# Packed attention with a SoLU MLP: the output stores move from the queue of SyncE to the queue of ScalarE

## The chip, the cores and the metric

The kernel runs on one core of a Trainium2 chip. The metric is the device time of one execution in microseconds; the three runs of the kernel before gave 470.54, 470.95 and 472.06, a median of 470.95. The profile was taken from one further execution of 470.67 us.

## The reference

What must be computed, cut to its core:

```python
def sm_attn(q, k, v):            # per batch and head, scale = 1/8
    s = scale * q @ k.T
    a = exp(s - max(s)); a = a / (sum(a) + 1e-9)
    return a @ v
packed = sm_attn(p, k, v)        # 32 packed rows for each of 8 batches and 8 heads
x = sm_attn(q, packed, packed)   # 576 rows for each batch, heads side by side: (4608, 512)
h = x @ w_in                     # (4608, 1024)
solu = h * softmax(h)
ln = (solu - mean(solu)) / sqrt(var(solu) + 1e-6) * g_ln
out = ln @ w_out                 # (4608, 512), float32
```

## The kernel before

The 4608 rows of the output are made in 36 tiles of 128 rows. There are 8 batches; four or five tiles belong to each, and a tile that straddles two batches takes its rows from both. In the text the tiles and their stores are counted from 0 to 35.

For each batch two generators spread attention work between the tiles of the MLP. `pack` (from L342) makes the 32 packed rows of a head: scores (L368), softmax (L373, L381), transposes of the exponentials on TensorE (L397) that ScalarE copies out of PSUM as `e1T` (L398), and the product with `v` (L407). `unpack` (from L419) makes the second attention with the input weights folded in: scores (L467), softmax (L443 to L451), the product of packed rows and `w_in` (L483), copied by ScalarE as `zh` (L485) with its rest `zl` (L500), and the transposed probabilities `a2h` and `a2l` (L505 to L508).

The MLP of a tile has three stages, each of a different step. `mlp_in` multiplies (L521), takes the row maximum on VectorE (L523), the exponential on ScalarE (L531) and `u` on VectorE (L534). `mlp_norm` subtracts the mean: `negmu` on GpSimd (L542), the upper half of `yhl` on ScalarE (L544), the lower half on VectorE (L545), a transposing DMA of `yhl` into `yT` that SyncE's queue issues (L547), and the sum of squares on ScalarE (L549), from which GpSimd makes `c_row` (L551 to L555). `mlp_out` multiplies `yT` with the halves of `w_out` (24 matmuls, L564), VectorE scales the result into `o_sb` (L566), and a pair of output rows and `o_sb` is put on the list `stores`.

`step` (L608) puts these together: `mlp_in` of a tile, `mlp_norm` of the tile before, then `store()`, which issues a DMA for what is on the list (the tile whose `mlp_out` came in the step before), then `mlp_out` of an earlier tile. Two more calls follow at the end.

All DMAs of the kernel are issued by SyncE's queue: the loads of `q` (L85, 16 of 72 KB for each of six batches), `k` (L96, four of 288 KB) and `v` (L107 and L134, two of 512 KB and one of 128 KB), the 36 transposes and the 36 stores of 256 KB. `raw` has three buffers, `v_sb` one, and `yhl`, `yT` and `o_sb` have two each.

The order of instructions on TensorE from the second batch on is that of the program. On the other engines and on SyncE's queue a planner orders them while it plays the program through in modelled time: by priorities (the offsets of `high_priority`) among what is ready. An engine then works through its list in order, and so an instruction that waits for a semaphore holds up what is behind it in that engine's list.

Of the kernel before, what the change touches and what calls it, by code (L numbers as in the profile page):

```python
# [38 lines left out]
def packed_attention_solu_kernel(ctx: ExitStack, tc: tile.TileContext, q: bass.AP, k: bass.AP, v: bass.AP, p: bass.AP, w_in: bass.AP, w_out: bass.AP, g_ln: bass.AP, out: bass.AP):  # L39
# [13 lines left out]
    nc = tc.nc  # L53
# [514 lines left out]

    def store():
        while stores:  # L570
            nc.sync.dma_start(*stores.pop(0))

    def run(work, n=None, offset=0):
        with tc.high_priority(offset=offset):
# [31 lines left out]
    normed, summed, stores = ([], [], [])  # L606

    def step(row, parts, knobs, work):  # L608
        lag, pout, pnorm = knobs
        before, after, mid = work  # L610
        before()
        nxt = mlp_in(row, parts)
        after()
        ready = normed.pop(0) if len(normed) > lag else None
        if summed:
            with tc.high_priority(offset=pnorm):
                normed.append(mlp_norm(*summed.pop()))
        store()
        if ready:
            with tc.high_priority(offset=pout):  # L620
                mlp_out(*ready, mid)
        else:
            mid()
        summed.append(nxt)
# [37 lines left out]
    for tile_ in normed:  # L662
        mlp_out(*tile_)
    store()
_INS = ['q', 'k', 'v', 'p', 'moe_w_in', 'moe_w_out', 'moe_g_ln']
_OUTS = [((4608, 512), 'float32')]
# [23 lines left out]
```

## Time and profile before

| what | value |
|---|---|
| median of 3 runs | 470.95 us (470.54 to 472.06) |
| the profiled execution | 470.67 us, of which the span is 468.9 us |
| TensorE busy (matmul) | 430.2 us, 92% |
| VectorE busy | 354.2 us, 76% |
| ScalarE busy | 232.4 us, 50% |
| GpSimd busy | 148.0 us, 32% |
| data DMAs, share of the 16 DMA engines | 74.3% |
| chain that ended last | TensorE 58%, VectorE 18%, DMA 10%, GpSimd 5% |

The span runs from the first to the last instruction; 1.8 us of the execution's time lie outside it. Engines are shortened as PE (TensorE's matmuls), PEld (its weight loads), DVE (VectorE), ACT (ScalarE), POOL (GpSimd) and SP (SyncE); a q behind a name, as in SPq, means the queue that issues DMAs. L571 is line 571 of the kernel. "out<-in" names the tiles that an instruction writes and reads. A figure in brackets at the end of a row is the idle time of the engine ahead of the instruction, with what ended it.

### The profile page before, as it was taken

Reading aid. Unit: us, or ns where it says so; the run is one execution under the profiler, and the core shown is the slowest. Engines: PE = TensorE matmul, PEld = TensorE weight load, DVE = VectorE, ACT = ScalarE, POOL = GpSimd, SP = SyncE. Lnnn points to the kernel's source line nnn. Section 1 sums busy time; section 2 is a strip of 40 time slices with the busy share of each in tenths; the row PEclk is TensorE's granted clock in tenths of the full one; section 3 lists DMA queues with packets and bytes.
Section 4 is the critical chain, followed back from the end, with each engine's and each line's share of the span. In section 5 each row is a group of like instructions: output and inputs, shape, how many; then the busy total and the mean of one; then the engine's idle time right before and its main releaser. Section 6 shows DMA issues by size and latency. Waiting matters only on the chain.

```text
span 468.9 us, 8271 instructions
## 1 busy us (share of the span) xinstructions
PE 430.2 (92%) x3116; PEld 234.7 (50%) x3116; DVE 354.2 (76%) x648; ACT 232.4 (50%) x404; POOL 148.0 (32%) x244
## 2 busy tenths in 40 slices
PE   9697795859979999999899998999999999999995
PEld 7472244633434555446544554566445555575552
DVE  3568989778768887988489979975898688655551
ACT  3577848654343653565244562653356536433430
POOL 3424556935103211421044123311342142111220
PEclk9979759988998999999999999999999999999999
DMA  9999999999569969965989588339035333526342
GB/s 265 336 268 286 152 207 124 135 193 155 110 138 185 169 127 181 191 142 95 204 111 135 109 177 154 89 69 214 23 68 113 69 69 83 119 67 134 70 101 78
DMA packets 237880, 67.00 MB, mean 143 GB/s; under 512 B 208912, under 2 KB 231440, under 8 KB 237328
## 3 DMA queue, kind: packets, MB, share of 16 engines
q1 hardware_dynamic: 237840, 66.48, 74.3%
q8 instruction: 24, 0.39, 0.4%
q14 instruction: 16, 0.13, 0.1%
HBM read 37.23 MB, written 9.44 MB: 100 GB/s over the span
## 4 chain that ended last, share of the span: by engine, by line
PE 58%; DVE 18%; DMA 10%; POOL 5%; issue 4%; SPq 2%; ACT 2%; DVEq 0%; ACTq 0%; POOLq 0%
PE po L564 30%; PE h L521 17%; DMA yT<-yhl 4%; DMA zh<-in_moe_w_in_dram 3%; PE pa L483 3%; PE pa L407 2%; PE pa L368 2%; DMA v_sb<-in_v_dram 2%; PE pa L397 2%; DVE yhl L545 2%; DVE nm L523 2%; DVE kT L350 2%; DVE u L534 1%; DMA p2raw<-in_p_dram 1%; PE pa L467 1%
## 5 line engine op out<-in xcount | busy, mean ns | idle before, releaser
L564 PE MATMUL po<-wch,yT 128*128 128x512 f16 x576 | 178.6, 380 | 4.5 <-DMA yT<-yhl 4.5
L564 PEld LDWEIGHTS <-yT 128*128 128x128 f16 x864 | 81.0, 98 | 116.5 <-issue 17.5
L564 PE MATMUL po<-wcl,yT 128*128 128x512 f16 x288 | 108.8, 379 | 0.0
L531 ACT ACTIVATE e<-h,nm 128x1024 f32<-128x1024 f32 x36 | 40.0, 1112 | 69.5 <-DVE nm L523 69.5
L521 PE MATMUL h<-zh,a2h 128*128 128x512 f32 x160 | 69.9, 437 | 1.7 <-DVE u L534 1.7
L544 ACT ACTIVATE yhl<-u,negmu 128x1024 f16<-128x1024 f32 x36 | 41.4, 1149 | 53.1 <-POOL negmu L542 51.2
L521 PE MATMUL h<-zl,a2h 128*128 128x512 f32 x160 | 64.2, 401 | 0.6 <-POOL zl L493 0.6
L521 PE MATMUL h<-zh,a2l 128*128 128x512 f32 x160 | 64.7, 404 | 0.0
L545 DVE SCALAR_TENSOR_TENSOR yhl<-u,negmu,yhl 128x1024 f16<-128x1024 f32 x36 | 48.5, 1346 | 15.5 <-ACT yhl L544 15.5
L523 DVE TENSOR_REDUCE nm<-h 128x1 f32<-128x1024 f32 x36 | 43.9, 1219 | 20.6 <-PE h L521 20.5
L534 DVE SCALAR_TENSOR_TENSOR u<-e,s_row,h 128x1024 f32<-128x1024 f32 x36 | 45.8, 1271 | 7.1 <-ACT e L531 5.0
L551 POOL TENSOR_SCALAR s_eps<-se,s_row 128x1 f32<-128x1 f32 x36 | 10.8, 301 | 110.9 <-ACT e L531 56.0
L554 POOL TENSOR_SCALAR c_row<-sq,s_eps 128x1 f32<-128x1 f32 x36 | 18.8, 521 | 78.9 <-ACT e L549 78.9
L549 ACT ACTIVATE e<-u,negmu 128x1024 f32<-128x1024 f32 x36 | 40.9, 1136 | 3.4 <-POOL negmu L542 3.4
L566 DVE SCALAR_TENSOR_TENSOR o_sb<-po,c_row,inv 128x512 f32<-128x512 f32 x36 | 26.7, 743 | 20.9 <-PE po L564 20.8
L521 PEld LDWEIGHTS h<-zh,a2h 128*128 128x128 f32 x160 | 31.2, 195 | 17.4 <-issue 8.2
L521 PEld LDWEIGHTS h<-zh,a2l 128*128 128x128 f32 x160 | 30.9, 193 | 8.7 <-DVE a2l L508 1.2
L521 PEld LDWEIGHTS h<-zl,a2h 128*128 128x128 f32 x160 | 31.0, 194 | 7.1 <-POOL zl L493 0.9
L485 ACT CAST zh<-pa 128x512 fp32r<-128x512 f32 x28 | 15.1, 583 | 23.3 <-PE pa L483 23.3
L444 POOL TENSOR_TENSOR s<-s,mx 128x576 f32<-128x576 f32 x14 | 16.9, 1229 | 30.2 <-DVE mx L443 30.1
L381 ACT ACTIVATE e<-pa,nmx 128x288 f32<-128x288 f32 x28 | 13.8, 499 | 21.6 <-DVE nmx L373 21.6
L221 POOL TENSOR_TENSOR u<-u 128x1024 fp32r<-128x1024 f32 (+1 forms) x5 | 12.9, 2573 | 28.3 <-ACT u L220 18.1
(138 smaller groups left out, 608.5 us busy)
## 6 DMA issues: line engine op xcount, KB each, us to landing
out_dram<-o_sb SPq DMA_DIRECT2D x36, 256.0 KB, 2.3
v_sb<-in_v_dram SPq DMA_DIRECT2D x16, 512.0 KB, 6.0
raw<-in_k_dram SPq DMA_DIRECT2D x28, 288.0 KB, 6.3
raw<-in_q_dram SPq DMA_DIRECT2D x96, 72.0 KB, 2.6
zh<-in_moe_w_in_dram SPq DMA_DIRECT2D x2, 1024.0 KB, 7.0
zl<-in_moe_w_in_dram SPq DMA_DIRECT2D x2, 1024.0 KB, 8.6
raw<-in_q_dram SPq DMA_DIRECT2D x4, 512.0 KB, 9.3
raw<-in_moe_w_out_dram SPq DMA_DIRECT2D x2, 1024.0 KB, 5.9
```

Source lines behind the costliest of these rows:

```text
L444: eng.tensor_tensor(out=s2[r], in0=s2[r], in1=mx.unsqueeze(2).broadcast_to([P, NB, J]), op=ALU.subtract)
L485: nc.scalar.copy(z_h[:, r, cols], pz)
L521: nc.tensor.matmul(h[:, 512 * n:512 * n + 512], lhsT=lhsT, rhs=z[:, r, 512 * n:512 * n + 512], start=t == 0, stop=t == len(terms) - 1)
L523: nc.vector.tensor_reduce(out=nm, in_=h, axis=AX.X, op=ALU.max, negate=True)
L531: nc.scalar.activation(e, h, AF.Exp, bias=nm, accum_out=se)
L534: nc.vector.scalar_tensor_tensor(out=u, in0=e, scalar=s_row, in1=h, op0=ALU.mult, op1=ALU.mult, accum_out=su)
L544: nc.scalar.activation(yhl[:, 0], u, AF.Identity, bias=negmu)
L545: nc.vector.scalar_tensor_tensor(out=yhl[:, 1], in0=u, scalar=negmu, in1=yhl[:, 0], op0=ALU.add, op1=ALU.subtract)
L549: nc.scalar.activation(e, u, AF.Square, bias=negmu, accum_out=sq)
L554: nc.gpsimd.tensor_scalar(out=c_row, in0=sq, scalar1=1.0 / DF, scalar2=s_eps, op0=ALU.mult, op1=ALU.add)
L564: nc.tensor.matmul(po, lhsT=yT[:, a, c], rhs=w[:, c], start=c == 0 and t == 0, stop=c == NFC - 1 and t == 2)
L566: nc.vector.scalar_tensor_tensor(out=o_sb, in0=po, scalar=c_row, in1=inv, op0=ALU.mult, op1=ALU.mult)
```

## The change

In `store()` the DMA is issued by `nc.scalar` and no longer by `nc.sync`. Nothing else differs: the same 36 transfers, from the same buffers to the same rows.

```diff
     def store():
         while stores:
-            nc.sync.dma_start(*stores.pop(0))
+            nc.scalar.dma_start(*stores.pop(0))
```

## Rows read from the trace of the kernel before

**Rows 1.** Busy time of each engine in two stretches of the span: start and end in us, length, busy us (instructions) of PE, PEld, DVE, ACT and POOL, granted TensorE clock as a share, mean share of the 16 DMA engines, GB/s.

```profile
120.00:455.00 335.00, 325.34 (x2330) 176.41 (x2329) 261.20 (x499) 158.57 (x275) 84.27 (x183) 0.99 0.64 121
455.00:468.90 13.90, 8.77 (x40) 3.64 (x38) 1.72 (x3) 0.00 (x0) 0.90 (x2) 1.00 0.35 91
```

**Rows 2.** The waits of the whole span, TensorE's weight loads and matmuls for the transposed tile: who waited for whom, us in total, times, longest us.

```profile
PEld L564 <- DMA yT<-yhl: 7.7, 5, 2.0
...
PE po L564 <- DMA yT<-yhl: 4.5, 4, 1.4
```

**Rows 3.** The line of the stores: instructions with duration in ns as min/median/max and the start of the first and the last in us; then the waits of SyncE's queue at that line.

```profile
L571 SPq DMA_DIRECT2D out_dram<-o_sb x36: 332/406/3612, 122.1 to 465.8; - x36
L571 SPq EVENT_SEMAPHORE  x26: 17/17/17, 121.0 to 459.6; - x26
...
SPq L571 <- DVE o_sb L566: 85.6, 16, 11.6
```

**Rows 4.** The timeline of TensorE's matmuls: start us, duration us, instruction, idle time before it. The three waits for a transpose between 120 and 455 us.

```profile
190.40 0.39 PE L564 MATMUL po<-wch,yT 128*128 128x512 f16 x1 [0.80 <-DMA yT<-yhl]
...
234.23 0.39 PE L564 MATMUL po<-wch,yT 128*128 128x512 f16 x1 [1.44 <-DMA yT<-yhl]
...
287.59 0.39 PE L564 MATMUL po<-wch,yT 128*128 128x512 f16 x1 [1.10 <-DMA yT<-yhl]
```

**Rows 5.** The timeline of SyncE's queue ahead of the first of these waits (neighbours of one kind merged: start us, us from the first to the end of the last, count). The stores are those of tiles 5 and 6, the transpose that of tile 7.

```profile
170.90 3.04 SPq L85 DMA_DIRECT2D raw<-in_q_dram  x6
174.04 0.44 SPq L571 DMA_DIRECT2D out_dram<-o_sb  x1
...
182.75 0.70 SPq L85 DMA_DIRECT2D raw<-in_q_dram  x1
183.56 3.47 SPq L547 DMA_TRANSPOSE yT<-yhl  x1
187.12 0.52 SPq L571 DMA_DIRECT2D out_dram<-o_sb  x1
```

**Rows 6.** The same queue ahead of the other two waits: the stores of tiles 9 and 14, the transposes of tiles 11 and 16.

```profile
217.11 0.43 SPq L571 DMA_DIRECT2D out_dram<-o_sb  x1
...
227.38 3.47 SPq L547 DMA_TRANSPOSE yT<-yhl  x1
...
270.92 0.44 SPq L571 DMA_DIRECT2D out_dram<-o_sb  x1
...
280.52 3.58 SPq L547 DMA_TRANSPOSE yT<-yhl  x1
```

**Rows 7.** Busy time by stretch, columns as in rows 1. In the first stretch a single store is all that the DMA engines move; the second follows the issue of tile 7's transpose.

```profile
446.40:448.20 1.80, 1.80 (x10) 1.22 (x9) 1.00 (x2) 0.12 (x2) 1.27 (x2) 1.00 0.39 146
...
184.70:188.70 4.00, 4.00 (x36) 2.54 (x42) 3.15 (x7) 0.00 (x0) 0.00 (x0) 1.00 1.32 228
```

**Rows 8.** The timelines of VectorE and of ScalarE around the three transposes of rows 5 and 6: `o_sb` of tiles 6 and 15 (the first and the last of three), and the next instruction of ScalarE behind each.

```profile
183.32 0.75 DVE L566 SCALAR_TENSOR_TENSOR o_sb<-po,c_row,inv 128x512 f32<-128x512 f32 x1 [0.71 <-PE po L564]
...
280.20 0.75 DVE L566 SCALAR_TENSOR_TENSOR o_sb<-po,c_row,inv 128x512 f32<-128x512 f32 x1 [0.71 <-PE po L564]
...
189.69 1.07 ACT L485 CAST zh<-pa 128x512 fp32r<-128x512 f32 x2 [7.26 <-PE pa L483]
...
286.57 1.07 ACT L485 CAST zh<-pa 128x512 fp32r<-128x512 f32 x2 [7.26 <-PE pa L483]
```

**Rows 9.** The timelines of VectorE, ScalarE and TensorE where `o_sb` is made while ScalarE copies `e1T`: tile 5 (the first of four such places, of tiles 5, 9, 14 and 18), tile 18 (the last of them), and tile 2.

```profile
172.60 0.74 DVE L566 SCALAR_TENSOR_TENSOR o_sb<-po,c_row,inv 128x512 f32<-128x512 f32 x1
...
312.58 0.74 DVE L566 SCALAR_TENSOR_TENSOR o_sb<-po,c_row,inv 128x512 f32<-128x512 f32 x1
...
314.37 1.14 ACT L549 ACTIVATE e<-u,negmu 128x1024 f32<-128x1024 f32 x1
...
315.50 0.57 ACT L398 COPY e1T<-pa 128x512 f32<-128x512 f32 x1
316.31 0.37 ACT L398 COPY e1T<-pa 64x256 f32<-64x256 f32 x1 [0.23 <-PE pa L397]
...
316.20 1.73 PE L407 MATMUL pa<-v_sb,e1T 128*32 128x64 f32 x80
...
134.12 0.75 DVE L566 SCALAR_TENSOR_TENSOR o_sb<-po,c_row,inv 128x512 f32<-128x512 f32 x1
...
134.90 1.45 ACT L398 COPY e1T<-pa 128x512 f32<-128x512 f32 x3 [0.71 <-PE pa L397]
```

**Rows 10.** The timelines of SyncE's queue, VectorE and ScalarE around the stores of tiles 7 and 11.

```profile
197.06 3.61 SPq L571 DMA_DIRECT2D out_dram<-o_sb  x1
...
195.91 0.65 DVE L566 SCALAR_TENSOR_TENSOR o_sb<-po,c_row,inv 128x512 f32<-128x512 f32 x1
...
196.82 1.15 ACT L544 ACTIVATE yhl<-u,negmu 128x1024 f16<-128x1024 f32 x1 [3.37 <-POOL negmu L542]
...
198.64 1.24 DVE L545 SCALAR_TENSOR_TENSOR yhl<-u,negmu,yhl 128x1024 f16<-128x1024 f32 x1
...
245.79 1.91 SPq L571 DMA_DIRECT2D out_dram<-o_sb  x1
...
242.34 0.74 DVE L566 SCALAR_TENSOR_TENSOR o_sb<-po,c_row,inv 128x512 f32<-128x512 f32 x1
...
243.60 1.05 ACT L485 CAST zh<-pa 128x512 fp32r<-128x512 f32 x2
```

## The prediction

> **What bounds the kernel now.** I read the busy time by stretch first. Stores run from 122.1 us to the end [rows 3], and between 120 and 455 us TensorE is busy 325.34 of 335 us at a granted clock of 0.99 [rows 1], so that stretch is TensorE's. All that a change of queues can win there are TensorE's pauses, 335 - 325.34 = 9.7 us (2%). Ahead of 120 us there are no stores. Behind 455 us ScalarE does nothing at all [rows 1], and the last store, at 465.8 us, ends the kernel.
>
> The list of waits then says what TensorE's pauses wait for. The transposed tile yT costs the matmuls 4.5 us in four waits, the longest 1.4 us; the weight loads, which run ahead of the matmuls, show longer ones for the same thing [rows 2]. Three of the four lie in the stretch: 0.80 + 1.44 + 1.10 = 3.34 us [rows 4]. The fourth (4.5 - 3.34, about 1.2 us) is that of the last tile, with no store ahead of it that could be cleared away. The other pauses, about 6 us, are the softmax chains between TensorE, VectorE and ScalarE.
>
> The timeline of SyncE's queue shows why the three are late: the transpose stands behind a burst of 16 loads of q and three of v, issued back to back from 170.90 us on, and in the middle of the burst sits a store of 0.44 us [rows 5]; the other two bursts have theirs at 217.11 and 270.92 us [rows 6]. The store that follows each transpose is the other thing to see there, because its data was ready earlier.
>
> **SyncE's queue: what is removed.** A store takes 0.41 us of the queue in the median, 36 of them 14.6 us [rows 3], but only those ahead of a transpose that TensorE waits for count. From the end of the sixth load (170.90 + 3.04 = 173.94) to the load behind the store lie about 0.1 us more than the store itself, and a part of that stays between any two DMAs: I take 0.49 us per burst, 3 x 0.49 = 1.5 us if each transpose lands as much earlier as it is issued. Each of the three waits is longer than 0.49, so none of it is cut off. SyncE's 85.6 us of waiting for o_sb [rows 3] are no loss today: it stands idle in most of them, and what it holds up there is not waited for by TensorE, or rows 2 would be longer.
>
> **The DMA engines: what is moved.** The same 256 KB stores now start when o_sb is there and ScalarE comes to them, not when SyncE does. For tile 6 o_sb ends at 183.32 + 0.75 = 184.07 us, and ScalarE has nothing until 189.69 us [rows 8]. Today SyncE issues that store at 187.12 us, behind tile 7's transpose (183.56 us) [rows 5]; after the change it goes out at about 184.1 us, beside it. The pattern is the same for the stores of tiles 10 and 15 [rows 6, 8]. While the transpose is on its way the DMA engines are full (their packets overlap to a share of 1.32), and one store alone takes 0.39 x 1.80 = 0.70 us of all sixteen [rows 7]. How a second queue is served beside the first no row shows, since all data goes through one queue now. If it gets its turn only afterwards the transpose loses nothing; if its packets come in between it loses up to 0.70 us. I take 0.70, as the store is issued before most of the transpose's packets can have moved. Per burst: 0.70 - 0.49 = +0.21 us, for three +0.6 us; bounds 3 x (-0.49) = -1.5 and, if the earlier issue is worth nothing to full engines, 3 x 0.70 = +2.1 us.
>
> The Trainium skill, "DMA: Bandwidth & Descriptors", section "Queues, rings and completion order", says that a DMA engine takes turns, packet by packet, between the queues that have work; by that the store would get in between, as I took it, and the sum would be +0.6. The same page's section "Issuing engines are not separate DMA queues" says that issuing from several engines "will only save the time on the sequencer it takes to initiate the DMA"; taken alone, that is the first lower bound, -1.5 us. The trace of before can show neither.
>
> **ScalarE: what is added.** 36 issues at 0.41 us are 14.6 us against 335 - 158.57 = 176 us of idle time [rows 1]; whether one costs anything depends on what stands behind it. The instructions that carry a store's data in come from VectorE, so the store adds a wait to ScalarE's list; I place each just behind the end of its o_sb. In most tiles ScalarE then idles for 1 us or more and the issue is covered. Exposed are the places where ScalarE is about to copy e1T, for which TensorE's product with v waits. There are four alike, tiles 5, 9, 14 and 18: o_sb ends (312.58 + 0.74 = 313.32) with two activations and two copies still to come, and the product starts at 316.20 us with no room for the last copy to be later [rows 9]. An issue shifts the third instruction by 0.41 us; the last copy has 0.23 us idle before it, so the cost lies between 0.18 and 0.41 us. For tiles 5, 9 and 14 it comes to nothing: TensorE then only reaches the next wait for yT later (0.80, 1.44 and 1.10 us long [rows 4]), and that wait's end is set by SyncE's burst. For tile 18 no such wait follows: 0.3 us. At tile 2 o_sb ends at 134.87 us, 0.03 us ahead of three copies [rows 9]: 0.41 us if the store is listed ahead of them, nothing behind; 0.2 us. Together +0.5, bounds 0 and 0.82 us.
>
> Semaphores beside the data: the short waits in front of 26 of the stores never lasted over 17 ns [rows 3], so I cost them at nothing; if ScalarE ran into one, its end would be the landing of an earlier DMA.
>
> The tail: ScalarE is idle behind 455 us, so the last two stores go out as promptly as from SyncE. Nothing.
>
> **Sum.** +0.6 + 0.5 = +1.1 us on the profiled execution's 470.67: 471.8 us, which is 0.2% above the median of the runs (470.95; the profiled one is 0.28 below it). A difference under 0.3%, 1.4 us, cannot be told from no change here. The likeliest case's own range, from the bounds, is 470.67 - 1.5 = 469.2 to 470.67 + 2.1 + 0.82 = 473.6 us.
>
> What no row prices is the planner: ScalarE's list gets 36 entries, SyncE's loses them, and neighbours on VectorE, ScalarE and GpSimd can change places. The pauses bound what can be won, 9.7 us; what can be lost is in the rivals.
>
> **Rivals.**
>
> Faster: the store's packets find gaps and the transposes keep the 0.49 us each, 470.67 - 1.5 = 469.2 us; if the emptier queue also lets a transpose pass loads, up to the whole 3.34 us goes, 467.3 us. I put it at 468.5. For it: the burst is back to back [rows 5], so every issue taken out counts. Against it: the full DMA engines [rows 7]. Chance 0.20.
>
> Slower, by an issue that holds ScalarE: on SyncE a store behind the loads of k took 3.61 us and another 1.91 [rows 10]. If ScalarE's issue is as slow while SyncE's loads are being issued, tile 7's store (o_sb ends at 196.56, L544 starts at 196.82) pushes L544 to about 200.2, and VectorE's L545 (198.64, 0.67 us behind the end of L544) by 3.35 - 0.67 = 2.7 us; tile 11's pushes the copy of zh by 243.08 + 1.91 - 243.60 = 1.4 us. With the 1.1 of the sum and some tenths elsewhere, +5 us: 475.7 us. It decides from an issue on ScalarE of about 1 us on. Against it: the 3.61 us may be the fullness of SyncE's own queue. Chance 0.22.
>
> Slower, by the planner's order: a store listed ahead of an instruction that the chip has ready earlier makes ScalarE wait for o_sb. One place too early costs up to an activation, 1.14 us [rows 9], and the issue; in some eight tiles ScalarE works through four or more instructions in a row around o_sb, and with half of it covered 8 x 0.8 = 6 us: 476.7 us. For it: on SyncE 16 stores were reached ahead of their data [rows 3]; against it: VectorE, which makes o_sb, is fed by the same activations. It decides where ScalarE's waits for o_sb pass 5 us in total. Chance 0.18.
>
> **How the numbers follow.** The forecast has 0.40. Of it 0.03 fall under 469.5 us, 0.32 within 1.4 us of 470.95, 0.05 above. The faster rival gives 0.16 and 0.04 to faster and same, the held ScalarE 0.02 and 0.20 to same and slower, the order 0.01 and 0.17. Sums: faster 0.19, same 0.39, slower 0.42. The range, 469.0 to 477.5 us, holds the likeliest case and both slow prices; about 0.1 is left out at either end.
>
> **What would show it.** Right: a second data queue with 9.4 MB; stores on ScalarE of 0.3 to 0.6 us; TensorE's three waits for yT of about 1.0, 1.65 and 1.3 us, with a store issued within a microsecond of each transpose; about 0.3 us ahead of the product with v near 316 us. Wrong: waits for yT shorter than 0.5 us, issues on ScalarE over 1 us, waits of ScalarE for o_sb of several microseconds, or pauses of TensorE at lines that had none, which would mean that the planner's new order and not the queue made the time.

## The result and the profile after

The changed kernel takes 473.92 us in the median of 20 runs (470.94 to 476.96), the kernel before 471.02 in 20 runs beside it (469.64 to 473.5). The ratio is 1.0063, with a 95% interval of 1.0048 to 1.0078: 0.6% or 2.9 us slower, where 471.8 us had been forecast. The profiled execution took 473.07 us with a span of 471.3 us, against 470.67 and 468.9: +2.4 us to be found in the trace. Among the runs below, one execution of e6_only_tile2, the profiled one, took 698.17 us at a mean granted clock of 0.557 and is left out, so that this run has no waits to show.

The page of the kernel after: busy time of each engine, the two data queues (packets, MB, share of the 16 DMA engines), the granted clock in 40 slices, and the stores.

```profile
PE 432.3 (92%) x3116; PEld 236.2 (50%) x3116; DVE 353.6 (75%) x648; ACT 232.6 (49%) x404; POOL 148.5 (32%) x244
...
PEclk9979757879997999999999999999999999999999
...
q1 hardware_dynamic: 232656, 57.04, 68.9%
q10 hardware_dynamic: 5184, 9.44, 5.6%
...
out_dram<-o_sb ACTq DMA_DIRECT2D x36, 256.0 KB, 2.5
```

The change did what it says: the 36 stores, 9.44 MB, have a queue of their own. No engine has more instructions; TensorE is still the one that is busy throughout. It is busy 2.1 us longer than before, but 1.6 us of that lie ahead of 118.6 us, where no store has been issued yet and the granted clock was 0.83 and not 0.86.

The busy time by stretch of the kernel after, columns as in [rows 1]:

```profile
120.00:455.00 335.00, 323.84 (x2322) 175.81 (x2320) 260.11 (x497) 157.10 (x273) 84.47 (x182) 0.99 0.65 121
```

In the same 335 us TensorE is busy 323.84 us and not 325.34 [rows 1], so its pauses grew by 1.5 us. Its waits for the transposed tile, as in [rows 2], and for `e1T`:

```profile
PEld L564 <- DMA yT<-yhl: 9.0, 5, 2.7
...
PE po L564 <- DMA yT<-yhl: 5.8, 4, 1.8
...
PEld pa L407 <- ACT e1T L398: 2.1, 7, 0.7
```

The matmuls wait 5.8 us for yT and not 4.5. The timeline of TensorE's matmuls shows where (tile 2's product with `v`, then the three waits of [rows 4]):

```profile
136.70 1.99 PE L407 MATMUL pa<-v_sb,e1T 128*32 128x64 f32 x80 [0.45 <-ACT e1T L398]
...
192.66 0.39 PE L564 MATMUL po<-wch,yT 128*128 128x512 f16 x1 [1.37 <-DMA yT<-yhl]
...
236.00 0.39 PE L564 MATMUL po<-wch,yT 128*128 128x512 f16 x1 [1.44 <-DMA yT<-yhl]
...
290.05 0.39 PE L564 MATMUL po<-wch,yT 128*128 128x512 f16 x1 [1.77 <-DMA yT<-yhl]
```

The three waits are 1.37 + 1.44 + 1.77 = 4.58 us against 3.34, so +1.24 us. The fourth, the last tile's, is 5.8 - 4.58 = 1.2 us as before. At tile 2 stands a pause of 0.45 us that the kernel before did not have; there the same line read:

```profile
136.02 1.73 PE L407 MATMUL pa<-v_sb,e1T 128*32 128x64 f32 x80
```

How late the same instruction is in the trace after adds up differently, since a delay can be taken up by the next wait:

| place | before, us | after, us | late by |
|---|---|---|---|
| L521, ahead of the first store | 118.58 | 118.88 | 0.30 |
| L407 of tile 2 | 136.02 | 136.70 | 0.68 |
| L564 of tile 7 | 190.40 | 192.66 | 2.26 |
| L564 of tile 11 | 234.23 | 236.00 | 1.77 |
| L564 of tile 16 | 287.59 | 290.05 | 2.46 |
| L407 near 316 us | 316.20 | 318.48 | 2.28 |
| span | 468.9 | 471.3 | 2.4 |

The first 0.30 us stand ahead of any store and are not of the change. About 1.0 us are added between 141 and 149 us, in a stretch at a lower granted clock that other executions have without the change (below). Of the rest the three transposes have the largest part.

SyncE's queue in the kernel after, unmerged for the transposes (as [rows 5, 6]):

```profile
172.59 8.16 SPq L85 DMA_DIRECT2D raw<-in_q_dram  x15
...
184.90 4.82 SPq L547 DMA_TRANSPOSE yT<-yhl  x1
...
192.86 6.33 SPq L96 DMA_DIRECT2D raw<-in_k_dram  x4
...
228.17 4.07 SPq L547 DMA_TRANSPOSE yT<-yhl  x1
...
282.07 4.16 SPq L547 DMA_TRANSPOSE yT<-yhl  x1
```

From the issue to the first matmul tile 7's transpose now needs 192.66 - 184.90 = 7.76 us, where it needed 190.40 - 183.56 = 6.84 [rows 4, 5]: +0.92. Tile 11's needs 7.83 and not 6.85 (+0.98), tile 16's 7.98 and not 7.07 (+0.91) [rows 4, 6]. It is not the next transpose that crowds them: that one follows 4.94, 4.20 and 4.27 us behind, where it was 4.19, 4.20 and 4.30. Their issues on SyncE's queue are longer too: 4.82, 4.07 and 4.16 us against 3.47, 3.47 and 3.58. What is issued beside them is to be seen in the line of the stores, as in [rows 3], and in ScalarE's timeline, which holds its activations and its queue's issues (ACTq):

```profile
L571 ACTq DMA_DIRECT2D out_dram<-o_sb x36: 338/338/382, 122.4 to 468.2; - x36
L571 ACTq EVENT_SEMAPHORE  x26: 17/17/17, 119.3 to 462.0; - x26
...
DMA to landing us min/median/max: 2.0/2.5/5.4
```

```profile
135.20 0.58 ACT L398 COPY e1T<-pa 128x512 f32<-128x512 f32 x1 [0.72 <-PE pa L397]
135.26 0.37 ACTq L571 DMA_DIRECT2D out_dram<-o_sb  x1
...
136.28 0.85 ACT L398 COPY e1T<-pa 64x256 f32<-64x256 f32 x2 [0.50 <-PE pa L397]
...
185.79 0.34 ACTq L571 DMA_DIRECT2D out_dram<-o_sb  x1
...
198.50 1.15 ACT L544 ACTIVATE yhl<-u,negmu 128x1024 f16<-128x1024 f32 x1 [3.37 <-POOL negmu L542]
198.83 0.34 ACTq L571 DMA_DIRECT2D out_dram<-o_sb  x1
...
315.60 1.15 ACT L544 ACTIVATE yhl<-u,negmu 128x1024 f16<-128x1024 f32 x1
315.66 0.34 ACTq L571 DMA_DIRECT2D out_dram<-o_sb  x1
316.65 1.14 ACT L549 ACTIVATE e<-u,negmu 128x1024 f32<-128x1024 f32 x1
```

Four things are to be seen. The store of tile 6 goes out at 185.79 us, 0.9 us behind tile 7's transpose, and no longer 3.56 us behind it [rows 5]. No issue on ScalarE takes more than 382 ns; tile 7's, which took 3.61 us on SyncE [rows 10], takes 0.34 at 198.83 us, while SyncE issues loads of `k` (from 192.86 us, for 6.33). An issue holds up no activation that is under way: that of 315.66 us lies inside L544 (315.60 to 316.75), and L549 follows at once. And at tile 2 the planner put things into another order: one large copy of `e1T`, the store, a small copy, and the second large copy last, where the three of [rows 9] were two large ones and then the small one. And no instruction of ScalarE starts late because of a store ahead of it: each follows the one before at once or is released by another engine, never by `o_sb`.

### The profile page after: what moved, and what is told of

Read it like the earlier page. It is cut to its first block, busy times and chain, and to the rows that moved or that the text cites. A ratio compares the mean times of both kernels' runs of the same rounds, so it can differ in the third digit from the quotient of the medians.

```text
span 471.3 us, 8266 instructions
## 1 busy us (share of the span) xinstructions
PE 432.3 (92%) x3116; PEld 236.2 (50%) x3116; DVE 353.6 (75%) x648; ACT 232.6 (49%) x404; POOL 148.5 (32%) x244
## 3 DMA queue, kind: packets, MB, share of 16 engines
q10 hardware_dynamic: 5184, 9.44, 5.6%
HBM read 37.23 MB, written 9.44 MB: 99 GB/s over the span
## 4 chain that ended last, share of the span: by engine, by line
PE 57%; DMA 12%; DVE 10%; SPq 6%; POOL 6%; issue 4%; ACT 3%; DVEq 0%; ACTq 0%; POOLq 0%
PE po L564 31%; PE h L521 17%; DMA yT<-yhl 7%; DMA zh<-in_moe_w_in_dram 3%; PE pa L407 2%; PE pa L483 2%; SPq L134 2%; SPq L85 2%; DMA raw<-in_k_dram 2%; PE pa L368 2%; PE pa L397 2%; DVE kT L350 2%; DVE yhl L545 1%; SPq L96 1%; SPq L107 1%
## 5 line engine op out<-in xcount | busy, mean ns | idle before, releaser
L564 PE MATMUL po<-wch,yT 128*128 128x512 f16 x576 | 178.8, 380 | 5.8 <-DMA yT<-yhl 5.8
L564 PEld LDWEIGHTS <-yT 128*128 128x128 f16 x864 | 80.9, 98 | 117.5 <-issue 17.3
L564 PE MATMUL po<-wcl,yT 128*128 128x512 f16 x288 | 109.0, 379 | 0.0
L521 PE MATMUL h<-zh,a2h 128*128 128x512 f32 x160 | 70.8, 442 | 1.0 <-DVE u L534 0.8
L544 ACT ACTIVATE yhl<-u,negmu 128x1024 f16<-128x1024 f32 x36 | 41.4, 1149 | 51.0 <-POOL negmu L542 49.1
L521 PE MATMUL h<-zh,a2l 128*128 128x512 f32 x160 | 65.6, 410 | 0.0
L521 PE MATMUL h<-zl,a2h 128*128 128x512 f32 x160 | 65.0, 406 | 0.6 <-POOL zl L493 0.6
L534 DVE SCALAR_TENSOR_TENSOR u<-e,s_row,h 128x1024 f32<-128x1024 f32 x36 | 45.7, 1271 | 7.0 <-ACT e L531 5.0
L549 ACT ACTIVATE e<-u,negmu 128x1024 f32<-128x1024 f32 x36 | 40.9, 1137 | 3.4 <-POOL negmu L542 3.4
L521 PEld LDWEIGHTS h<-zh,a2h 128*128 128x128 f32 x160 | 31.6, 198 | 17.2 <-issue 6.6
L521 PEld LDWEIGHTS h<-zh,a2l 128*128 128x128 f32 x160 | 31.4, 196 | 8.9 <-DVE a2l L508 0.9
L521 PEld LDWEIGHTS h<-zl,a2h 128*128 128x128 f32 x160 | 31.5, 197 | 7.3 <-POOL zl L493 0.9
L221 POOL TENSOR_TENSOR u<-u 128x1024 fp32r<-128x1024 f32 (+1 forms) x5 | 12.9, 2576 | 27.9 <-ACT u L220 17.5
```

The source lines that it names most:

```text
L521: nc.tensor.matmul(h[:, 512 * n:512 * n + 512], lhsT=lhsT, rhs=z[:, r, 512 * n:512 * n + 512], start=t == 0, stop=t == len(terms) - 1)
L534: nc.vector.scalar_tensor_tensor(out=u, in0=e, scalar=s_row, in1=h, op0=ALU.mult, op1=ALU.mult, accum_out=su)
L544: nc.scalar.activation(yhl[:, 0], u, AF.Identity, bias=negmu)
L549: nc.scalar.activation(e, u, AF.Square, bias=negmu, accum_out=sq)
L564: nc.tensor.matmul(po, lhsT=yT[:, a, c], rhs=w[:, c], start=c == 0 and t == 0, stop=c == NFC - 1 and t == 2)
```

## The experiments

The first theory was the prediction's: three stores now move beside three transposes and delay them by more than the emptier queue gives back. Its rivals were the new order at tile 2, a changed burst of loads, and the granted clock. All runs number the stores as they are issued and choose the queue by the number; only the condition differs:

```diff
+            n = len(stored)
+            stored.append(n)
+            eng = nc.sync if <condition> else nc.scalar
-            nc.scalar.dma_start(*stores.pop(0))
+            eng.dma_start(*stores.pop(0))
```

Each is timed against the kernel before on the same chip. The waits are TensorE's for yT at tiles 7, 11 and 16, in one profiled execution of each, together 3.34 us before.

| run | on ScalarE's queue | ratio, 95% interval | median us (before) | waits, us |
|---|---|---|---|---|
| e0_after | all | 1.0059 (1.0039 to 1.0079) | 473.8 (471.11) | 5.04 |
| e1_three_back | all but 6, 10, 15 | 1.0013 (1.0001 to 1.0024) | 471.88 (471.11) | 2.79 |
| e2_tile2_back | all but 2 | 1.0027 (1.0008 to 1.0046) | 472.29 (471.11) | 5.08 |
| e3_four_back | all but 2, 6, 10, 15 | 1.0007 (0.999 to 1.0023) | 471.55 (471.11) | 2.03 |
| e4_only_three | 6, 10, 15 | 1.0085 (1.0051 to 1.0118) | 475.33 (471.12) | 6.61 |
| e10_three_again | 6, 10, 15 | 1.0057 (1.0038 to 1.0077) | 474.34 (471.45) | 7.21 |
| e7_halves | half of each of 6, 10, 15 | 1.0031 (1.0015 to 1.0046) | 472.37 (471.12) | 4.60 |
| e5_only_bursts | 5, 9, 14 | 0.999 (0.997 to 1.001) | 470.76 (471.12) | 2.73 |
| e11_bursts_again | 5, 9, 14 | 0.9984 (0.9967 to 1.0) | 470.91 (471.45) | 2.79 |
| e6_only_tile2 | 2 | 1.0034 (1.0013 to 1.0054) | 472.44 (471.12) | none |
| e8_tile2_again | 2 | 1.0017 (1.0001 to 1.0033) | 472.21 (471.45) | 3.79 |

**The change once more (e0_after).** No edit; it shows how far two profiles of one kernel differ.

> The changed kernel once more, as the yardstick of the others on this chip. Theory (two places): TensorE's waits for yT near 192, 236 and 290 us are about 1.4, 1.4 and 1.8 us, the product with v near 136 us starts with a wait of about 0.45 us for the last copy of e1T, ratio to before about 1.006. Rival (clock): the time follows the granted clock, and runs with a mean clock of 0.96 are as fast as the kernel before (471).

The ratio repeats (1.0059), and the three waits are 5.04 us where the first profile had 4.58. A sum of three waits is thus known to about half a microsecond, and a single one less well: they are 1.01, 1.86 and 2.17 us here, and a further wait for yT, 0.75 us at 257.80 us, is one that the first profile does not have.

**The three stores beside the transposes back on SyncE (e1_three_back).**

```diff
+            eng = nc.sync if n in (6, 10, 15) else nc.scalar
```

> The stores of tiles 6, 10 and 15, those beside the late transposes, go back to SyncE; the other 33 stay on ScalarE. Contention theory: the three transposes take 6.8 to 7.0 us from issue to landing again (7.7 to 7.9 in the changed kernel) and are still issued earlier, so the three waits fall below those of before (0.80, 1.44, 1.10), to about 0.5, 0.6 and 0.9 us; the wait of 0.45 us at 136 us stays; about 1.5 to 2.5 us faster than the changed kernel, ratio to before about 1.001 to 1.002. Rival (clock, or the 36 issues themselves): ratio stays at 1.005 or more.

Three stores of 36 take the ratio from 1.0059 to 1.0013 and the waits from 5.04 to 2.79 us, while the pause at tile 2 stays (0.46 us at 137.08). So most of the loss hangs on these three: 1.9 us of the 2.7 by the medians (473.8 to 471.88).

**Tile 2's store back, and all four back (e2_tile2_back, e3_four_back).**

```diff
+            eng = nc.sync if n == 2 else nc.scalar
...
+            eng = nc.sync if n in (2, 6, 10, 15) else nc.scalar
```

> Only tile 2's store goes back to SyncE, so the planner's order of the e1T copies at 135 us and of L534 and L508 on VectorE is that of before. Theory (two places): the wait of 0.45 us in front of the product with v is gone and the waits for yT stay at 1.4, 1.4 and 1.8 us; 0.5 to 1 us faster than the changed kernel, ratio about 1.004. Rival (clock): the pause at 136 us is what lengthens the stretch at half clock near 142 us from 3.4 to 6.8 us; then that stretch is 3.4 us again and the gain is 1.2 us or more.

> The stores of tiles 2, 6, 10 and 15 go back to SyncE, 32 stay on ScalarE. Theory (two places): nothing of the loss is left and the earlier issue of the three transposes is kept, 0.3 to 0.9 us each: waits for yT of about 0.5, 0.6 and 0.9 us, ratio to before 0.996 to 0.999. Rival (the 36 issues cost by themselves, or the clock): ratio 1.002 or more.

With tile 2's store alone back, L407 has no pause (it starts at 136.02 us, as in the kernel before), the waits for yT stay at 5.08 us, and the ratio is 1.0027. The 1.5 us that this gains by the medians are more than the pause and more than was expected; the rival, that the clock falls less without the pause, asked for 1.2 us or more and is not refuted by this run alone (see the part on the clock at the end). With all four back the ratio is 1.0007, which cannot be told from no change; the 0.996 to 0.999 that were expected from the earlier issue did not come. The three waits in the timeline of e3_four_back, and one at L368:

```profile
157.08 1.31 PE L368 MATMUL pa<-kT,pT 64*32 64x288 f32 x16 [1.06 <-DVE zl L500]
...
190.64 0.39 PE L564 MATMUL po<-wch,yT 128*128 128x512 f16 x1 [0.64 <-DMA yT<-yhl]
...
233.62 0.39 PE L564 MATMUL po<-wch,yT 128*128 128x512 f16 x1 [0.43 <-DMA yT<-yhl]
...
286.87 0.39 PE L564 MATMUL po<-wch,yT 128*128 128x512 f16 x1 [0.96 <-DMA yT<-yhl]
```

They are 1.3 us shorter than before together, but TensorE waits 1.06 us for VectorE at 157.08 us. That wait is not of the stores: it stands in the profiles of e1_three_back, e2_tile2_back, e3_four_back and e5_only_bursts (0.82 to 1.07 us), the four in which the granted clock stayed up near 142 us, and in no other.

**The three stores alone on ScalarE (e4_only_three, e10_three_again).** The burst keeps its stores, and 33 stores stay where they were.

```diff
+            eng = nc.sync if n not in (6, 10, 15) else nc.scalar
```

> Only the stores of tiles 6, 10 and 15 go to ScalarE; the other 33 stay on SyncE, those in the middle of the bursts too. Contention theory: the transposes are issued no earlier than before and take 0.5 to 1.4 us longer to land, so the three waits grow to about 1.5, 2.1 and 2.2 us (5.8 in all against 3.3), ratio to before about 1.005. Rival (it is the 36 issues on ScalarE, or the planner's new order): three issues cost nothing, ratio 1.000.

> The stores of tiles 6, 10 and 15 alone on ScalarE once more, as six runs gave a wide interval (1.0051 to 1.0118) and more than the whole change. Contention theory: waits for yT of about 1.8, 2.2 and 2.6 us again, 6.6 us in all against 3.3 of before, ratio 1.006 to 1.009. Rival (those six runs were a chance): ratio 1.002 to 1.004.

They cost as much as the whole change or more: ratios of 1.0085 and 1.0057. The waits of e10_three_again, with tile 7's transpose (the first of two merged here) and the store beside it:

```profile
184.47 7.72 SPq L547 DMA_TRANSPOSE yT<-yhl  x2
...
184.95 0.39 ACTq L574 DMA_DIRECT2D out_dram<-o_sb  x1
...
192.81 0.61 PE L564 MATMUL po<-wch,yT 128*128 128x512 f16 x1 [2.39 <-DMA yT<-yhl]
...
238.18 0.39 PE L564 MATMUL po<-wch,yT 128*128 128x512 f16 x1 [1.95 <-DMA yT<-yhl]
...
293.31 0.39 PE L564 MATMUL po<-wch,yT 128*128 128x512 f16 x1 [2.87 <-DMA yT<-yhl]
```

Tile 6's store goes out 0.48 us behind the transpose, and the waits grow from 3.34 to 7.21 us, 1.29 us for each store (1.09 in e4_only_three). Of all transposes the longest time from issue to landing is 9.0 us here, 7.9 in the changed kernel and 7.5 in the kernel before. This profile is of the slowest of the 12 executions (476.25 us). Part of its time, and of e4_only_three's, is the granted clock. Behind the wait of 2.39 us it is 0.50:

```profile
192.60:195.90 3.30, 3.09 (x8) 1.16 (x9) 3.30 (x11) 1.70 (x4) 0.76 (x3) 0.50 1.30 217
```

The matmul that starts at 192.81 us is 2.41 us later than before (190.40), the one at 196.08 us 3.95 us (192.13). In e4_only_three it is the same behind the wait of 2.19 us, from 236.3 to 239.6 us. The two profiles of the changed kernel have no such fall behind 150 us, so these two runs, as far as one profile of each tells, overstate what the three stores cost in it.

**Half of each store (e7_halves).** Of the three stores the first 256 columns go out from ScalarE's queue, the rest from SyncE's; all others from SyncE's.

```diff
+            if n in (6, 10, 15):
+                nc.scalar.dma_start(dst[:, :256], src[:, :256])
+                nc.sync.dma_start(dst[:, 256:], src[:, 256:])
+            else:
+                nc.sync.dma_start(dst, src)
```

> As the kernel with only the stores of tiles 6, 10 and 15 on ScalarE, but only half of the columns of each (128 KB) goes there; the other half stays on SyncE behind the transpose. Contention theory: the price goes with the bytes that pass beside the transpose, so the waits grow half as much, to about 1.2, 1.8 and 1.7 us, ratio 1.002 to 1.003. Rival (any DMA of another queue beside a transpose holds it up, whatever its size): waits as with the whole stores.

The ratio is 1.0031, between a third and somewhat over a half of what the whole stores cost; the waits grow by 4.60 - 3.34 = 1.26 us, about a third of their 3.27 and 3.87. ScalarE's queue has 432 packets in all three runs, 0.39 MB here and 0.79 MB there. So the price goes with the bytes that move beside the transpose, not with the fact that a second queue issues something, nor with its packets.

**The stores in the bursts alone (e5_only_bursts, e11_bursts_again).** What the emptier queue gives back by itself.

```diff
+            eng = nc.sync if n not in (5, 9, 14) else nc.scalar
```

> Only the stores of tiles 5, 9 and 14, those in the middle of the bursts of loads, go to ScalarE. Theory (the issue time saved on SyncE is worth what it takes there): the three transposes are issued 0.4 to 0.5 us earlier and land in 6.8 to 7.0 us, waits of about 0.4, 1.0 and 0.7 us, 1.0 to 1.5 us faster than before, ratio 0.997 to 0.998. Rival (full DMA engines: the earlier issue is worth nothing, or the store's bytes still stand in the way): waits as before, ratio 1.000.

> The stores of tiles 5, 9 and 14 alone on ScalarE once more, to see whether it beats the kernel before: theory 0.998 to 0.999 with waits for yT of 2.7 us in all, rival 1.000.

The three waits in the timeline of e5_only_bursts:

```profile
190.47 0.39 PE L564 MATMUL po<-wch,yT 128*128 128x512 f16 x1 [0.58 <-DMA yT<-yhl]
...
233.82 0.39 PE L564 MATMUL po<-wch,yT 128*128 128x512 f16 x1 [0.73 <-DMA yT<-yhl]
...
287.45 0.39 PE L564 MATMUL po<-wch,yT 128*128 128x512 f16 x1 [1.42 <-DMA yT<-yhl]
```

They are 0.61 us shorter than before together (0.55 in e11_bursts_again), and the ratios are 0.999 and 0.9984. A gain of 1.0 to 1.5 us had been expected; this is one of 0.1 to 0.2%, and the intervals reach to 1: these two runs are the only kernels not above the kernel before in the median, and that they beat it isn't shown.

**Tile 2's store alone (e6_only_tile2, e8_tile2_again).**

```diff
+            eng = nc.sync if n != 2 else nc.scalar
```

> Only tile 2's store goes to ScalarE. Theory (the planner then lists the small copy of e1T ahead of the second large one, and TensorE's product with v waits for the large one): a wait of about 0.45 us at 136 us, all else as before; ratio 1.001 to 1.002. Rival (that pause brings the granted clock down behind it): a stretch of 6.8 us at half clock near 142 us and a mean clock of 0.952 over the runs, ratio 1.003 or more.

> Tile 2's store alone on ScalarE once more, for a profile at full clock. Theory (copies listed in another order): TensorE waits 0.45 us for e1T in front of the product with v near 136 us, and the swap of L534 and L508 on VectorE shows as a longer wait of L368 for zl near 205 us (0.07 us before, 0.9 us where 33 stores were on ScalarE and the swap was there); waits for yT as before; ratio 1.002 to 1.004. Rival (clock): no other wait grows and the stretch at half clock near 142 us is 6.8 us long.

One store costs 0.34% and 0.17%. The timelines of ScalarE and of TensorE at tile 2, in e8_tile2_again:

```profile
134.34 0.59 ACT L398 COPY e1T<-pa 128x512 f32<-128x512 f32 x1 [0.72 <-PE pa L397]
134.40 0.40 ACTq L574 DMA_DIRECT2D out_dram<-o_sb  x1
135.42 0.85 ACT L398 COPY e1T<-pa 64x256 f32<-64x256 f32 x2 [0.50 <-PE pa L397]
...
135.84 1.99 PE L407 MATMUL pa<-v_sb,e1T 128*32 128x64 f32 x80 [0.46 <-ACT e1T L398]
```

The pause is the same as with all 36 stores moved. It does not come from the issue of 0.40 us, which ends inside the first copy: ScalarE idles 0.50 us ahead of the next copies, and they come in the new order, the small one ahead, which has to wait for TensorE. A wait of some 0.9 us near 205 us that had been expected there, from the order of L534 and L508 on VectorE that changes with this store too, did not appear. The rival of the clock fits e6_only_tile2 (1.0034, a mean granted clock of 0.954 where 1.003 or more and 0.952 had been put down for it) and not e8_tile2_again (1.0017 and 0.962, though in its profile the clock is 0.54 from 141.6 to 148.6 us), so these two runs leave it open.

## Why the prediction was right, and by what

**Held.** The time lies in the range (469.0 to 477.5 us), and "slower by over 0.3%" had the largest chance, 0.42. The likeliest case named the mechanism: each of three transposes meets a store on the DMA engines that used to follow it, and loses more than the burst of loads gives back. e1_three_back, e4_only_three, e10_three_again and e7_halves show it from both sides. By the Trainium skill, "DMA: Bandwidth & Descriptors", section "Queues, rings and completion order", a DMA engine takes turns by packet between the queues that have work. That the transposes need 0.91 to 0.98 us longer with a store of the other queue beside them agrees with it. The same page's "Issuing engines are not separate DMA queues", by which only issue time is saved, agrees with the bursts alone: 0.55 to 0.61 us of waits, and no time that can be told from none.

**Luck.** Of the 0.42 only 0.05 came from the likeliest case, whose forecast, 471.8 us, was a change too small to be told from none; 0.37 came from the two slower rivals, and both fell. The likeliest case's own range ended at 473.6 us, and 473.92 lies just outside it: what holds it is the room that was left for those rivals. The mechanism was right; its size was not.

**The step that failed** is the size of the term for the DMA engines: "I take 0.70, as the store is issued before most of the transpose's packets can have moved. Per burst: 0.70 - 0.49 = +0.21 us, for three +0.6 us". It is the 0.70 us that was too small: the store's own time of all sixteen engines [rows 7] is no upper bound of what a transpose loses to it. In the changed kernel the transposes lost 0.92, 0.98 and 0.91 us, 2.81 in place of 2.1, and the waits, forecast as about 1.0, 1.65 and 1.3 us, came out as 1.37, 1.44 and 1.77, tile 11's no longer than before. One profile says little of one transpose, but the twelve together agree: from issue to landing the three take 7.5, 7.5 and 8.5 us on average in the five profiles with a whole store beside them (the kernel after, e0_after, e2_tile2_back, e4_only_three, e10_three_again) and 6.5, 6.9 and 7.0 us in the six with the store behind them, so 1.0 us more.

The other side, 0.49 us per burst, holds on average, though not from one pair of profiles to the next. From the first load to the transpose it is 13.1, 13.5 and 12.9 us on average in the five profiles with the burst's store on SyncE's queue and 12.4, 12.8 and 12.7 us in the seven without, 0.5 us less; but profiles of one kind differ by up to 1.2 us. For tile 7 it is 184.90 - 172.59 = 12.31 us in the changed kernel, 12.50 in e11_bursts_again and 12.81 in e5_only_bursts, against 183.56 - 170.90 = 12.66 before [rows 5]. With 1.0 in place of 0.70 the three bursts come to +1.5 us; where the prediction had +0.63 us in the three waits, the traces show +1.24 and, in e0_after, +1.70.

**ScalarE, tile 2: wrong cause.** "0.41 us if the store is listed ahead of them, nothing behind; 0.2 us." It is 0.45 us, near the first of the two, but it comes from the planner's exchange of two copies, not from the issue's time. It costs 0.2 to 0.3% alone (e6_only_tile2, e8_tile2_again), some 1 us, more than the pause; where the rest goes stays open. A pause of TensorE at a line that had none was also one of the signs of being wrong, and this is one, though a small one.

**Tile 18: wrong.** The forecast 0.3 us ahead of the product near 316 us is nothing. "An issue shifts the third instruction by 0.41 us" does not hold where the issue can run beside an activation, as it does at 315.66 us.

**Nothing lost, as forecast:** the semaphores (17 ns) and the tail (last wait 1.2 us in both).

**The rivals.** The faster one fell: the waits are longer. The issue that holds ScalarE fell: it decides from about 1 us, and no issue took over 0.382. That ScalarE waits for `o_sb` fell: no instruction of it is released by `o_sb`. Of the planner's order only tile 2 is left.

**The sum from the runs.** Putting three stores back takes 1.0059 - 1.0013 = 0.46 points of the 0.59. The rest, 0.13, fits tile 2 (0.17 to 0.34) less the bursts (0.10 to 0.16). Made alone, the three cost 0.57 to 0.85 points, so the parts do not simply add: with the bursts' stores moved as well, the waits are shorter (4.58 to 5.08 us) than without (6.61 to 7.21); and the two profiles without have the further fall of the clock.

**The clock.** One microsecond of the profile's difference is not explained by any wait. The busy time by stretch from 141.6 to 148.6 us, columns as in [rows 1], of the kernel after:

```profile
141.60:148.60 7.00, 6.39 (x39) 2.87 (x38) 5.66 (x11) 1.29 (x3) 1.41 (x2) 0.51 1.09 215
```

of the kernel before:

```profile
141.60:148.60 7.00, 6.44 (x32) 3.41 (x33) 6.81 (x12) 2.23 (x4) 2.28 (x2) 0.76 1.01 194
```

of e1_three_back:

```profile
141.60:148.60 7.00, 6.26 (x49) 3.23 (x50) 6.16 (x12) 1.40 (x3) 1.52 (x2) 1.00 1.03 211
```

and of e10_three_again and e5_only_bursts, in this order:

```profile
141.60:148.60 7.00, 6.43 (x33) 3.60 (x27) 6.69 (x11) 2.07 (x4) 2.28 (x2) 0.53 1.01 207
...
141.60:148.60 7.00, 6.38 (x44) 3.38 (x38) 6.55 (x11) 1.94 (x4) 2.27 (x2) 1.00 1.00 204
```

The granted clock is 0.51 in the kernel after, which is the lower of its two levels (1.2 and 2.4 GHz) for nearly the whole stretch, 0.76 before and 1.00 in e1_three_back, and TensorE is busy for 6.3 to 6.4 of the 7 us in all five. That is the 1.0 us of the profile's 2.4 that no wait explains. Neither the change nor the pause at tile 2 is needed for it: up to 141 us e10_three_again and e5_only_bursts run the same instructions as the kernel before, on every engine in the same order, and the clock is 0.53 in the one and 1.00 in the other, while e1_three_back has the pause and no fall. So this microsecond of one profile cannot be put down to the change. Where the clock stays up TensorE waits about 1 us more at L368 near 157 us (e3_four_back), which gives most of it back.

**What stays open** is the clock over many runs. The mean is 0.952 over the runs of the kernel after and 0.958 over those of the kernel before that stood beside the experiments. In e4_only_three and e10_three_again it fell behind one long wait for yT each, and not behind the longest ones, of 2.60 and 2.87 us; how often that happens in the changed kernel, and how much of its 2.9 us it is, one profile of each run does not tell.

## What to carry to other kernels

A second queue takes an issue off the first, but it also takes away an order: look for what the moved transfers used to stand behind, and whether someone waits for that. When a transfer is let loose beside one that an engine waits for, count its whole time on the DMA engines as lost there, and somewhat more (here 1.0 us for 0.70); an issue saved from a queue counts for little if what follows it waits for buffers. If anything is to be won, it is with the transfers that stand ahead of the awaited one, and those behind it stay; here even that gain (0.1 to 0.2%) isn't shown.

## What the runs showed of the hardware that was not expected

In the changed kernel an issue on ScalarE takes 338 to 382 ns and runs while the activation before it is still at work (315.66 us inside 315.60 to 316.75), so that most of the 36 cost ScalarE nothing. A store that took 3.61 us to issue behind loads on its own queue [rows 10] took 0.34 on the other at the same place, with the first queue's loads still being issued: that speaks for the fullness of its own queue, and not of the DMA engines, as the cause of the long issue. And with a 256 KB store beside it a transpose's own issue took 4.82, 4.07 and 4.16 us in place of 3.47, 3.47 and 3.58 [rows 5, 6] (not everywhere: tile 7's stayed at 3.50 us in e4_only_three), and its way to the matmul 0.91 to 0.98 us more, which is more than the 0.70 us in which the sixteen engines move the store by itself.
